# Group norm on one core: the last store of each run cut into four quarters by partitions, with waits between them, and ScalarE's loop left unaligned

## The chip, the cores and the metric

The kernel runs on one core of a Trainium2 chip. The metric is device time in microseconds (us) of one execution, lower is better. The kernel before takes 633.49 us (median of three runs, 633.39 to 634.88).

## The reference

Group norm over x of shape (128, 1024, 32, 16) in bf16, with 32 groups of 32 channels. Each of the 128 x 32 groups has 32 x 512 = 16384 values. Cut to what matters:

```python
xr  = x.reshape(B, 32, C // 32, H, W)
mu  = xr.mean(axis=(2, 3, 4), keepdims=True)
var = ((xr - mu) ** 2).mean(axis=(2, 3, 4), keepdims=True)
xn  = ((xr - mu) / jnp.sqrt(var + 1e-5)).reshape(B, C, H, W)
return xn * g[None, :, None, None] + b[None, :, None, None]
```

x is 134.2 MB and is read once; the output has the same size and is written once.

## The kernel before, in words

**Tiles.** A tile holds four samples: 4 x 32 groups lie on the 128 partitions, and each partition has the 16384 bf16 values (32 KB) of one group. A tile is 4 MB, and there are 32 of them (NT = 32). They go through six buffers in SBUF, xt0 to xt5 (NBUF = 6); tile i is in buffer i % 6. The result is written over the input in the same buffer and stored from there.

**Engines.** For each tile TensorE (L142) sums the 32 slices of 512 columns into one PSUM tile by 32 matmuls with the identity matrix. VectorE reduces that to the negative mean (L161). ScalarE makes two passes of Square with accumulation over halves of the tile (L255), then two small activations that give the standard deviation (L269, L276). VectorE takes the reciprocal (L174), forms a scale and a bias for each of the 32 channels of a group (L177, L184) and applies them by 32 instructions in place (L194). Its last instruction adds one to the semaphore s_dve.

**Loops.** TensorE, VectorE and ScalarE each run two tiles unrolled, and then a hardware loop of five trips with six tiles in its body. This is the helper `loop` (L90 to L106). It hands the loop `head_slot={engine.engine: 0}`: the loop's first instruction is loaded at slot 0 of an instruction fetch block, and a branch leads over the padding.

**SyncE and the DMA order.** All large transfers are issued by SyncE, in `sync_program` (L108 to L123), which is fully unrolled. A transfer is one tile of 128 partitions. SyncE works through its list in order, so a wait in it holds back all that stands behind it. Six loads go first. Then for each tile i SyncE waits until VectorE is done with it (s_dve, L119) and issues its store (L120), which adds 16 to the buffer's semaphore st on landing. After every third store (RUN = 3; i = 1, 4, 7, ... 25) it issues the loads of the next run, and ahead of each it waits for the landing of the store that last used the buffer (L112, L113):

```python
def load(i):
    j = i % NBUF
    if i >= NBUF:
        sync.wait_ge(st[j], 16 * (i // NBUF))
    sync.dma_start(out=xt[j][:], in_=x_v[i]).then_inc(ld[j], 16)
```

So the order is: six loads, two stores, two loads, and then three stores and three loads in turn; after the load of tile 31 come the last six stores. There are nine places at which a run of stores is followed by loads. ScalarE issues two small loads of g and b at the start.

Of the kernel before, what the change touches and what calls it, by code (L numbers as in the profile page):

```python
# [17 lines left out]
NBUF = 6  # L18
RUN = 3
# [5 lines left out]
def kernel(  # L25
# [8 lines left out]
    P = nc.NUM_PARTITIONS  # L34
# [6 lines left out]
    NT = B0 // NS  # L41
# [8 lines left out]
    o_v = out.rearrange("(t n) (g k) h w -> t (n g) (k h w)", n=NS, g=G)  # L50
# [6 lines left out]
    xt = [sb.tile([P, F], BF16, name=f"xt{j}") for j in range(NBUF)]  # L57
# [19 lines left out]
    def sem(name):  # L77
        return tc.alloc_semaphore(name)

    ld = [sem(f"ld{j}") for j in range(NBUF)]  # L80
    st = [sem(f"st{j}") for j in range(NBUF)]
    s_gb, s_set, s_eye, s_rep = sem("s_gb"), sem("s_set"), sem("s_eye"), sem("s_rep")
    s_pe, s_mean, s_sq, s_std = sem("s_pe"), sem("s_mean"), sem("s_sq"), sem("s_std")
    s_dd, s_dve = sem("s_dd"), sem("s_dve")

    def col(t, i):
        j = i % NBUF
        return t[:, j : j + 1]

    def loop(engine, step, settle, counts):  # L90


        for i in range(HEAD):
            step(i)
        with nc.Fori(
            0,
            TRIPS,
            1,
            engines=bass.OrderedEngineSet([engine.engine]),
            head_slot={engine.engine: 0},  # L100
        ):
            for i in range(HEAD, HEAD + NBUF):
                step(i)
            settle()
            for s, n in counts:
                engine.sem_inc(s, -n)  # L106

    def sync_program(sync):  # L108
# [3 lines that stand above are left out]
                sync.wait_ge(st[j], 16 * (i // NBUF))  # L112
            sync.dma_start(out=xt[j][:], in_=x_v[i]).then_inc(ld[j], 16)  # L113

        for i in range(min(NBUF, NT)):
            load(i)
        for i in range(NT):
            j = i % NBUF
            sync.wait_ge(s_dve, i + 1)  # L119
            sync.dma_start(out=o_v[i], in_=xt[j][:]).then_inc(st[j], 16)  # L120
            if (NT - NBUF - 1 - i) % RUN == 0:
                for n in range(max(NBUF, i + 1 + NBUF - RUN), min(i + 1 + NBUF, NT)):
                    load(n)  # L123

    def tensor_program(pe):
        pe.wait_ge(s_gb, 32)
        pe.wait_ge(s_rep, 1)
        pe.matmul(  # L128
            out=gb_p[:].rearrange("p a k -> p (a k)"),
            lhsT=rep[:],  # L130
            rhs=gb_b[:].rearrange("q a k -> q (a k)"),
            start=True,
            stop=True,
        ).then_inc(s_pe, 1)
        pe.wait_ge(s_eye, 1)

        def step(i):
            j = i % NBUF
            pe.wait_ge(ld[j], 16)
            pe.sem_inc(ld[j], -16)  # L140
            for k in range(NMM):
                m = pe.matmul(  # L142
                    out=pa[j][:],
                    lhsT=eye[:],
                    rhs=xt[j][:, k * MM_FREE : (k + 1) * MM_FREE],
                    start=(k == 0),
                    stop=(k == NMM - 1),
                )
            m.then_inc(s_pe, 1)

        loop(pe, step, lambda: None, [])
        pe.drain()
        pe.sem_inc(s_pe, 1)

    def vector_program(dve):
# [52 lines left out]
        def settle():  # L208
            dve.wait_ge(s_dd, 3 * (HEAD + NBUF) + 2)

        mean(0)
        loop(
            dve,
            step,
# [31 lines left out]
    def scalar_program(act):  # L246
        act.dma_start(out=gb_b[:, 0, :], in_=g_v).then_inc(s_gb, 16)
        act.dma_start(out=gb_b[:, 1, :], in_=b_v).then_inc(s_gb, 16)
        act.wait_ge(s_set, 2)
        act.activation(out=warm[:], in_=eps_t[:], func=ACT.Sqrt)  # L250

        def step(i):
            j = i % NBUF
            for h in range(2):
                m = act.activation(  # L255
                    out=ja[:],
                    in_=xt[j][:, h * F // 2 : (h + 1) * F // 2],
                    func=ACT.Square,
                    bias=col(negmean, i),
                    scale=1.0,  # L260
                    accum_out=sq[:, 2 * j + h : 2 * j + h + 1],
                    saturate=False,
                )
                if h == 0:
                    m._wait_ge(s_mean, i + 1)
                else:
                    m._wait_ge(s_sq, 3 * i + 1)
                m.then_inc(s_sq, 1)
            act.activation(  # L269
                out=col(half, i),  # L270
                in_=sq[:, 2 * j : 2 * j + 1],
                func=ACT.Identity,
                bias=eps_t[:],
                scale=inv_n,
            )._wait_ge(s_sq, 3 * i + 1).then_inc(s_sq, 1)
            act.activation(  # L276
                out=col(std, i),
                in_=sq[:, 2 * j + 1 : 2 * j + 2],
                func=ACT.Sqrt,
                bias=col(half, i),  # L280
                scale=inv_n,
            )._wait_ge(s_sq, 3 * i + 3).then_inc(s_std, 1)

        loop(act, step, lambda: act.drain(), [(s_mean, NBUF), (s_sq, 3 * NBUF)])

    with tc.tile_critical():  # L286
        with nc.Block() as block:
            block.sync(sync_program)
            block.tensor(tensor_program)
            block.vector(vector_program)  # L290
            block.gpsimd(pool_program)
            block.scalar(scalar_program)

        for j in range(NBUF):
            nc.sync.wait_ge(st[j], 16 * len(range(j, NT, NBUF)))
# [30 lines left out]
```

## Time and profile before

| | |
|---|---|
| median of three runs | 633.49 us |
| time of the profiled execution | 632.89 us |
| its span, first to last instruction | 631.1 us |
| moved to and from HBM | 134.22 MB read, 134.22 MB written, 425 GB/s over the span |
| busy: TensorE | 260.1 us, 41% |
| busy: VectorE | 375.6 us, 60% |
| busy: ScalarE | 476.2 us, 75% |
| load, issue to landing (median) | 29.1 us |
| store, issue to landing (median) | 33.3 us |

The profile is that of one execution. Its page gives busy times, the span in 40 equal slices (each digit is a busy share in tenths), the DMA queues, the chain of work that ended last, and groups of instructions by source line with the mean duration of one in nanoseconds. The trace behind it answers who waited for whom, prints instructions in order of time, and records every DMA packet with its start, duration and size, and the landing of every transfer. Times in the trace count from the span's start. SyncE has no busy time: all that it does is wait and issue.

### The profile page before, as it was taken

The numbers are of one execution on the slowest core, as the hardware profiler recorded it, in microseconds if no ns is written. First come the engines' busy times: TensorE is split into PE (matmuls) and PEld (weight loads), VectorE is DVE, ScalarE is ACT, GpSimd is POOL, SyncE is SP. The second block draws the span as 40 slices with busy tenths as digits, with TensorE's granted clock in tenths as the row PEclk, the third lists the DMA queues.
The fourth block names the chain that finished last, engine by engine and source line by source line (L and its number), as shares of the span: only waits on it lengthen the run. The fifth ranks groups of instructions, "written<-read, shape, count | busy, mean of one in ns | idle before, by whom it ended". The sixth has DMA issues, their size and how long they took to land. (4 is left out here: it accounts for less than half of the span.)

```text
span 631.1 us, 3670 instructions
## 1 busy us (share of the span) xinstructions
PE 260.1 (41%) x1025; PEld 106.2 (17%) x1025; DVE 375.6 (60%) x1188; ACT 476.2 (75%) x194; POOL 0.9 (0%) x7
## 2 busy tenths in 40 slices
PE   1877409008602750572087018604720670095000
PEld 0333103003201310230032003201310230032000
DVE  0067477774772777077627745770777177447771
ACT  0596999996994699199819965993899199749940
POOL 0000000000000000000000000000000000000000
PEclk9988858658855975687578659755975796588555
DMA  8999999999999999999999999999999999999996
GB/s 366 431 432 402 434 434 432 435 432 432 430 432 434 434 432 434 432 432 434 432 432 430 432 434 430 432 434 432 426 436 434 434 428 434 432 436 432 432 397 287
DMA packets 9320, 268.53 MB, mean 425 GB/s; under 512 B 1120, under 2 KB 1120, under 8 KB 1120
## 3 DMA queue, kind: packets, MB, share of 16 engines
q1 hardware_dynamic: 9216, 268.44, 99.0%
q14 instruction: 6, 0.05, 0.0%
q8 instruction: 2, 0.03, 0.0%
q10 hardware_dynamic: 96, 0.00, 0.0%
HBM read 134.22 MB, written 134.22 MB: 425 GB/s over the span
## 5 line engine op out<-in xcount | busy, mean ns | idle before, releaser
L255 ACT ACTIVATE ja<-xt,negmean 128x8192 fp8e5<-128x8192 bf16 x64 | 455.5, 7117 | 127.1 <-DVE jd L161 120.6
L142 PE MATMUL pa<-xt,eye 128*128 128x512 bf16 x1024 | 259.9, 419 | 309.1 <-PEq L140 306.9
L194 DVE TENSOR_SCALAR xt<-xt,scl,bia 128x512 bf16<-128x512 bf16 x1024 | 333.6, 405 | 1.2
L142 PEld LDWEIGHTS pa<-xt,eye 128*128 128x128 bf16 x1024 | 106.1, 106 | 462.5 <-issue 368.8
L161 DVE TENSOR_SCALAR_CACHE_REDUCE jd<-pa 128x512 bf16<-128x512 f32 x33 | 22.6, 685 | 144.6 <-PE pa L142 142.8
L174 DVE RECIPROCAL rstd<-std 128x1 f32<-128x1 f32 x32 | 5.2, 162 | 82.9 <-ACT std L276 82.9
L255 ACT ACTIVATION_READ_ACCUMULATOR ja<-xt,negmean 128x1 f32 x64 | 11.9, 186 | 0.0
L276 ACT ACTIVATE std<-sq,half 128x1 f32<-128x1 f32 x32 | 9.4, 294 | 1.0
L269 ACT ACTIVATE half<-sq,eps_t 128x1 f32<-128x1 f32 x32 | 8.9, 278 | 0.0
L184 DVE SCALAR_TENSOR_TENSOR bia<-scl,negmean,gb 128x32 f32<-128x32 f32 x32 | 8.0, 251 | 1.1
L177 DVE TENSOR_SCALAR scl<-gb,rstd 128x32 f32<-128x32 f32 x32 | 7.7, 242 | 1.1
L157 DVE COPY gb<-gb_p 128x64 f32<-128x64 f32 x1 | 0.2, 225 | 9.8 <-PE gb_p L128 9.8
L128 PE MATMUL gb_p<-gb_b,rep 32*128 32x64 bf16 x1 | 0.2, 231 | 10.8 <-DMA gb_b<-in_b_dram 10.8
L250 ACT ACT_TABLE_LOAD x1 | 1.3, 1283 | 1.9 <-issue 1.9
L161 DVE DVE_READ_ACCUMULATOR jd<-pa 128x1 f32 x33 | 2.7, 81 | 0.0
L128 PEld LDWEIGHTS gb_p<-gb_b,rep 32*128 32x128 bf16 x1 | 0.1, 100 | 10.8 <-DMA gb_b<-in_b_dram 10.8
L156 DVE MEMSET ones_b<- 128x128 bf16 x1 | 0.2, 165 | 1.1 <-SPq L286 1.1
L229 POOL TENSOR_SCALAR_AFFINE_SELECT rep<-ones_b 32x128 bf16<-32x128 bf16 x1 | 0.3, 305 | 0.0
L220 POOL TENSOR_SCALAR_AFFINE_SELECT eye<-ones_b 128x128 bf16<-128x128 bf16 x1 | 0.3, 294 | 0.8 <-DVE ones_b L156 0.8
L250 ACT ACTIVATE warm<-eps_t 128x1 f32<-128x1 f32 x1 | 0.2, 203 | 0.0
L238 POOL TENSOR_SCALAR eps_t<-ones_b 128x1 f32<-128x1 bf16 x1 | 0.2, 204 | 0.0
L310 POOL MEMSET const-bfloat16-1.0<- 128x1 bf16 x1 | 0.1, 102 | 0.0
(3 smaller groups left out, 0.3 us busy)
## 6 DMA issues: line engine op xcount, KB each, us to landing
xt<-in_x_dram SPq DMA_DIRECT2D x32, 4096.0 KB, 29.1
out_dram<-xt SPq DMA_DIRECT2D x32, 4096.0 KB, 33.3
gb_b<-in_g_dram ACTq DMA_DIRECT2D x1, 2.0 KB, 6.1
gb_b<-in_b_dram ACTq DMA_DIRECT2D x1, 2.0 KB, 9.3
```

Source lines behind the costliest of these rows:

```text
L128: pe.matmul(out=gb_p[:].rearrange("p a k -> p (a k)"), lhsT=rep[:], rhs=gb_b[:].rearrange("q a k -> q (a k)"), start=True, stop=True,).the ...
L142: m = pe.matmul(out=pa[j][:], lhsT=eye[:], rhs=xt[j][:, k * MM_FREE : (k + 1) * MM_FREE], start=(k == 0), stop=(k == NMM - 1),)
L161: dve.tensor_scalar(out=jd[i % 2][:], in0=pa[i % NBUF][:], scalar1=-inv_n, scalar2=None, op0=ALU.mult, op1=ALU.add, accum_out=col(negmean, i),
L174: dve.reciprocal(out=col(rstd, i), in_=col(std, i))._wait_ge(s_std, i + 1).then_inc(s_dd, 1)
L177: dve.tensor_scalar(out=scl[j][:], in0=gam, scalar1=col(rstd, i), scalar2=None, op0=ALU.mult,)._wait_ge(s_dd, 3 * i + 2).then_inc(s_dd, 1)
L184: dve.scalar_tensor_tensor(out=bia[j][:], in0=scl[j][:], scalar=col(negmean, i), in1=bet, op0=ALU.mult, op1=ALU.add,)._wait_ge(s_dd, 3 * i ...
L194: m = dve.tensor_scalar(out=span, in0=span, scalar1=scl[j][:, k : k + 1], scalar2=bia[j][:, k : k + 1], op0=ALU.mult, op1=ALU.add,)
L220: pool.affine_select(out=eye[:], in_=ones_b[:], pattern=[[-1, P]], compare_op=ALU.is_equal, fill=0.0, base=0, channel_multiplier=1,)._wait ...
L250: act.activation(out=warm[:], in_=eps_t[:], func=ACT.Sqrt)
L255: m = act.activation(out=ja[:], in_=xt[j][:, h * F // 2 : (h + 1) * F // 2], func=ACT.Square, bias=col(negmean, i), scale=1.0, accum_out=s ...
L269: act.activation(out=col(half, i), in_=sq[:, 2 * j : 2 * j + 1], func=ACT.Identity, bias=eps_t[:], scale=inv_n,)._wait_ge(s_sq, 3 * i + 1) ...
L276: act.activation(out=col(std, i), in_=sq[:, 2 * j + 1 : 2 * j + 2], func=ACT.Sqrt, bias=col(half, i), scale=inv_n,)._wait_ge(s_sq, 3 * i + ...
```

## The change

Two edits.

In `sync_program`, the store at each of the nine places where loads follow (i = 1, 4, ... 25) is replaced by four stores of 32 partitions each, 1 MB, with three new semaphores qt0 to qt2. The first two quarters are issued together; the third is issued when the first has landed, and the fourth when the second has landed. The fourth adds to st as the whole store did. Then SyncE waits for the landing of the third, and goes on to the loads, whose own waits are as before. The other 23 stores stay whole.

In `loop`, ScalarE's loop is built without `head_slot`: its body is loaded right behind the unrolled part, wherever in a block that is. The instructions of the body are the same, and those of the other engines are all as before.

```diff
+    qt = [sem(f"qt{c}") for c in range(3)]
...
-    def loop(engine, step, settle, counts):
+    def loop(engine, step, settle, counts, aligned=True):
...
-            head_slot={engine.engine: 0},
+            **({"head_slot": {engine.engine: 0}} if aligned else {}),
...
+        def gated(i):
+            return i < NT - NBUF and (NT - NBUF - 1 - i) % RUN == 0
+
+        def store_in_quarters(i):
+            j = i % NBUF
+            q = P // 4
+            n = 16 * (gates[0] + 1)
+            gates[0] += 1
+            for c in range(4):
+                if c >= 2:
+                    sync.wait_ge(qt[c - 2], n)
+                rows = slice(c * q, (c + 1) * q)
+                sync.dma_start(out=o_v[i][rows], in_=xt[j][rows]).then_inc(
+                    qt[c] if c < 3 else st[j], 16
+                )
+            sync.wait_ge(qt[2], n)
+
+        gates = [0]
...
-            sync.dma_start(out=o_v[i], in_=xt[j][:]).then_inc(st[j], 16)
+            if gated(i):
+                store_in_quarters(i)
+            else:
+                sync.dma_start(out=o_v[i], in_=xt[j][:]).then_inc(st[j], 16)
...
-        loop(act, step, lambda: act.drain(), [(s_mean, NBUF), (s_sq, 3 * NBUF)])
+        loop(act, step, lambda: act.drain(), [(s_mean, NBUF), (s_sq, 3 * NBUF)], aligned=False)
```

## The prediction

> **What bounds the kernel now.** I read the page's DMA part first, then the windows by stage, then SyncE's waits and its timeline, and the chain last. On the page the DMA row, the rate row and the queue row:
>
> ```profile
> DMA  8999999999999999999999999999999999999996
> GB/s 366 431 432 402 434 434 432 435 432 432 430 432 434 434 432 434 432 432 434 432 432 430 432 434 430 432 434 432 426 436 434 434 428 434 432 436 432 432 397 287
> q1 hardware_dynamic: 9216, 268.44, 99.0%
> ```
>
> The reader is to see nines from the second slice to the last but one, and 426 to 436 from the fifth slice to the third from the end: SyncE's queue keeps the 16 DMA engines busy for 99% of the span. 9216 packets are 144 a transfer: 128 rows of 32 KB and 16 short ones that report completion. In the trace's packet records 95 of 100 rows take 1213 to 1219 ns, load or store alike, so one engine moves 27.0 GB/s, and a transfer (8 rows an engine) takes 8 x 1.213 = 9.70 us. Landings do follow each other by 9.69 us. Two windows, one steady cycle of three loads and three stores and the stretch before the first store (columns: length, busy time of each engine, clock, DMA share, GB/s):
>
> ```profile
> 53.20:64.40 11.20, 8.75 (x32) 3.50 (x32) 10.98 (x34) 6.59 (x1) 0.00 (x0) 0.85 1.00 383
> 249.10:307.90 58.80, 24.34 (x96) 9.99 (x96) 35.90 (x114) 45.24 (x19) 0.00 (x0) 0.73 1.00 431
> ```
>
> In the cycle DMA is full (1.00), while ScalarE, the busiest engine, has 45.2 of 58.8 us. So whatever lengthens the DMA work of a cycle lengthens the kernel by as much, and compute has 13 us a cycle to spare. What keeps DMA full is depth in the queue, seen in SyncE's timeline of a cycle (start, length from first issue to last, line):
>
> ```profile
> 221.26 0.33 SPq L120 DMA_DIRECT2D out_dram<-xt  x1
> 229.80 19.65 SPq L113 DMA_DIRECT2D xt<-in_x_dram  x3
> 249.50 30.17 SPq L120 DMA_DIRECT2D out_dram<-xt  x3
> ```
>
> and in its waits (who <- for what: us in total, times, longest):
>
> ```profile
> SPq L120 <- DVE xt L194: 368.3, 23, 44.6
> SPq L113 <- DMA out_dram<-xt: 223.3, 25, 10.1
> ```
>
> The run's last store is issued at 221.26 with two stores ahead of it and lands at 249.11. The next loads are issued at 229.80, 239.50 and 249.12, on the landings of the three stores, so the first load stands 19 us in the queue before its data can flow. At the end, the chain:
>
> ```profile
> 607.00 10.42 DVE xt L194 x32
> ```
>
> VectorE ends at 617.42, the last store is issued at 617.44, and the store ahead of it lands at 619.51: compute and DMA reach the end within about a microsecond of each other (15 DMA engines write their last row until 628.0, one until 628.86). Both chains start at the landings of the last three loads, so a delay ahead of those goes to the end in full.
>
> **The change part by part.** All sums are against the profiled execution, 632.89 us, which lies 0.6 us under the median of 633.49.
>
> *Bytes and packets.* Nothing is removed: a quarter is 32 rows. The two small loads of g and b, also 32 rows, show how such a transfer is spread: 64 data packets and 32 completion packets for the two, so 32 and 16 each, two rows on every one of 16 engines. The nine places have 27 more issues and 27 x 16 completion packets of 9 ns, three to an engine and place: under 0.3 us in all, and the issues (0.33 us) lie beside data. Nothing.
>
> *The waits.* SyncE now waits for a first quarter, a second and a third; behind it stand the remaining quarters, the loads, and the next run's stores. The next stores are not late: before, SyncE came to them at the landing of the whole store (249.50) as well, and three loads (29 us) then cover them. The loads lose their 19 us of cover and keep one quarter. The price of a hand-over, from the end of one quarter's data to the first packet of the next, in the rows: completion packet to landing 0.34 to 0.46 us, landing to SyncE's issue 0.01 (store landed 249.11, load issued 249.12), issue to first packet 1.02 (first load, 1.00 to 2.02): 1.4 us. The worst row is the g load, issue 0.96 to first packet 3.93, behind other data: 2.97, in all 3.4. The cover is the quarter that is still in flight, at least 2 x 1.213 = 2.43 us. So at 1.4 us nothing shows; at 3.4 us it costs 3 hand-overs x 1.0 us x 9 = 27 us.
>
> *The length of a quarter.* This decides. Lower end: each engine keeps its 1213 ns a row, a quarter takes 2.43 us, four take 9.70, as the whole store did: zero. But a whole store has the 16 engines reading 16 sets of eight rows, and a quarter has them all reading within 32 partitions. No transfer of size in the trace does that. Loads write SBUF and read HBM, stores do the reverse, and both run at 1213 ns: the limit is not HBM's reading or writing but the engine's own, or that of its way into SBUF. If it is the way, two engines that meet on one share it: 2 x 1.213 = 2.43 us a row, 4.85 a quarter, 19.41 for four against 9.69, 9.72 more at each of nine places: **+87.5 us**. Upper end: the slowest row in the records, 2.508 us (at 58.8, in the 383 GB/s window above, where many engines slow down at once): 5.02 a quarter, 20.06 for four, +10.4 x 9 = +93 us. I take 4.85, the doubled row; its row of 2.43 us is nearest to the slow rows that the trace does have, 2.1 to 2.5 us. In it the hand-overs are covered by 4.85 us.
>
> [...]
>
> *ScalarE's loop.* At the loop's entry ScalarE stands idle, with nothing that released it:
>
> ```profile
> 52.06 0.29 ACT L276 ACTIVATE std<-sq,half 128x1 f32<-128x1 f32 x1
> 57.81 7.12 ACT L255 ACTIVATE ja<-xt,negmean 128x8192 fp8e5<-128x8192 bf16 x1 [5.45 <-issue]
> ```
>
> Two 8 KB instruction packets run at 56.1. Without the jump up to 5.45 us go from ScalarE's path; tile 2's store is next held by SyncE, which issues it at 84.12, right behind a load at 83.74, and DMA is full throughout: zero. On the other side, a body that straddles two blocks could stall as long at each of four back edges. ScalarE waits there 5.0 us (146.8) and 13.4 to 13.6 (from 254.6 on) for VectorE anyway, which covers it but for 0.45 us that DMA does not see. Were that cover gone, in the last cycle, it would be 5.45 us. Value: zero.
>
> **Sum**: 632.89 + 87.5 = **720.4 us**.
>
> **Rivals.**
>
> *No change.* The rows keep 1213 ns, because the limit is the engine's own. Then 9.70 against 9.69 at each place, hand-overs of 1.4 us under 2.43: 633 us. For it: 27.0 GB/s in all rows of both directions. Against: it asks that 32 partitions feed 16 engines as 128 do.
>
> *Faster* (the other side). The engines drift apart: the completion packets of the store that landed at 249.11 are spread over 3.05 us, of that at 542.07 over 5.46. The third load of a run lands late, by 0.69, 0.77, 0.40 and 0.40 us (278.88, 395.9, 454.46, 513.03), when the leading engines are already at stores; one landing at 123.27 is 0.77 late. A gate stops the leaders until the last engine has landed a quarter, and closes the spread at each of nine places, while the last engine always has a quarter in hand. If the late landings come from the spread, 3.0 us go: 629.9 us. It decides only where a quarter lasts under 2.43 + 3.0 / 36 = 2.51 us. Against: the late loads come only at some of the places, while the spread is there at all.
>
> *Hand-overs uncovered.* Rows at full rate, but a hand-over near 3.4 us: 633 + 27 = 660 us. Against: the 3.4 is behind another queue's rows.
>
> **How the numbers follow.** The doubled row 0.58 (by itself 705 to 732: down to 0.83 x 87.5 = 73 us more, if drift keeps two engines of a way apart for a sixth of the rows, and up to 726 plus one ScalarE stall of 5.45), hand-overs or a row in between 0.08, no change 0.16, faster 0.18. About 0.3% (1.9 us) is what a measurement of this kernel can tell from no change. Faster 0.18, same 0.16, slower 0.66. The likeliest alone holds too little, so the range reaches over the cases between and no change to the edge of the faster one, 630, and up to 732.
>
> **What would show it.** In the profile after: DMA share stays near 1.00 while the rate falls to about half in a stretch of some 19 us at each place, and SyncE's wait between the second and third quarter is near 4.85 us. A flat 430 with waits of 2.43 us would be no change; then the spread and the third loads' landings tell of the faster rival. A DMA share under 0.9 ahead of the loads would be uncovered hand-overs. The prediction is wrong if a row of a quarter stays at 1213 ns.

## The result, and the profile after

The kernel after takes 722.12 us (median of six runs, 719.67 to 726.4) against 633.92 us before (six runs): a ratio of 1.1397, 95% interval 1.1355 to 1.1439. The forecast was 720.4 us. The profiled execution after has 724.91 us and a span of 723.2 us, 92.1 us more than the span before; all that follows is told against these two spans.

The DMA row, the rate row and the queue row of the page after:

```profile
DMA  9999999999999999999999999999999999899997
GB/s 377 434 433 404 241 411 425 270 341 419 435 219 379 406 430 228 417 426 370 259 431 430 317 314 428 410 299 338 428 431 241 391 433 393 219 428 406 435 433 323
q1 hardware_dynamic: 9648, 268.44, 98.0%
```

The DMA row is still nines but for one 8 and the last slice, and the rate row is no longer flat: it dips at nine places, to between 219 and 314, one for each cut store. The DMA engines are nearly as busy as before and move about half as much there. A busy share alone would not have shown this; share and rate have to be read together. The 432 added packets (9648 against 9216) are the completions.

One place by windows, after (columns: length, busy time of each engine, clock, DMA share, GB/s): the four quarters, from the landing of the store ahead of them to their own last landing; within that, the last quarter; then the first load behind them.

```profile
270.80:287.80 17.00, 0.00 (x0) 0.00 (x0) 11.09 (x35) 15.12 (x8) 0.00 (x0) 0.50 0.94 220
283.80:287.90 4.10, 0.00 (x0) 0.00 (x0) 0.00 (x0) 2.18 (x4) 0.00 (x0) 0.50 0.76 216
287.80:299.60 11.80, 0.00 (x0) 0.00 (x0) 0.00 (x0) 0.00 (x0) 0.00 (x0) 0.50 0.99 394
```

A whole last store, and the first load behind it, in the kernel before:

```profile
239.50:249.10 9.60, 0.00 (x0) 0.00 (x0) 8.95 (x29) 9.54 (x5) 0.00 (x0) 0.50 1.01 437
249.10:258.80 9.70, 0.00 (x0) 0.00 (x0) 2.13 (x7) 5.74 (x4) 0.00 (x0) 0.50 1.00 432
```

The same 4 MB take 17.0 us at 220 GB/s where they took 9.6 at 437. The load behind them takes 11.8 instead of 9.7. A window counts each packet whole at its start, so share and rate of a short one are rough, and shares over 1 occur. The 0.76 of the last quarter leaves out rows that began before it. With every row counted by the part of it that lies inside, the engines are 0.91 busy there and idle for 0.4 us; in the whole 17.0 us they are idle for 0.5.

SyncE's timeline at this place, and its waits for landings in the whole span (us in total, times, longest):

```profile
252.41 26.66 SPq L130 DMA_DIRECT2D out_dram<-xt  x4
283.78 4.40 SPq L114 DMA_DIRECT2D xt<-in_x_dram  x3
```

```profile
SPq L130 <- DMA out_dram<-xt: 220.2, 18, 25.7
SPq L114 <- DMA out_dram<-xt: 59.4, 18, 4.8
```

The first load is now issued at 283.78, when the third quarter has landed, 4.1 us before the last one lands; before, it was issued 19 us ahead.

ScalarE at its loop's entry, after:

```profile
52.99 0.29 ACT L300 ACTIVATE std<-sq,half 128x1 f32<-128x1 f32 x1
53.20 7.11 ACT L279 ACTIVATE ja<-xt,negmean 128x8192 fp8e5<-128x8192 bf16 x1
```

The 5.45 us stall is gone.

**Where the 92 us are.** The landing records give a sum. Over the nine places the quarters take 67.8 us more than whole stores at 9.69 us would (17.2 us a place); the first loads behind them land 18.7 us late in all (2.1 each); all other landings together are 5.5 us later than before; the first load lands 0.3 us later. That is 92.3, the difference of the spans to 0.2 us. The packet records give a second sum, per DMA engine: 512 rows at 1.213 us are 621.1 us; rows that took longer added 3.0 us before and 86.7 after; time with no row in work was 2.8 us before and 11.5 after. Before, nearly all of that lies at the end, where engines that are ahead wait for the last store, issued at 617.44; after, 8.8 us of it lie at the nine places. So about nine tenths are slow rows, and one tenth is idle time. 580 rows took 2.50 to 2.60 us (the quarters have 1152); before, one did.

### The profile page after: what moved, and what is told of

Read it like the earlier page. It is cut to its first block, busy times and chain, and to the rows that moved or that the text cites. A ratio compares the mean times of both kernels' runs of the same rounds, so it can differ in the third digit from the quotient of the medians.

```text
span 723.2 us, 3705 instructions
## 1 busy us (share of the span) xinstructions
PE 259.1 (36%) x1025; PEld 105.8 (15%) x1025; DVE 375.8 (52%) x1188; ACT 476.1 (66%) x194; POOL 0.9 (0%) x7
## 3 DMA queue, kind: packets, MB, share of 16 engines
q1 hardware_dynamic: 9648, 268.44, 98.0%
## 5 line engine op out<-in xcount | busy, mean ns | idle before, releaser
L279 ACT ACTIVATE ja<-xt,negmean 128x8192 fp8e5<-128x8192 bf16 x64 | 455.5, 7116 | 217.9 <-DVE jd L185 216.9
L152 PE MATMUL gb_p<-gb_b,rep 32*128 32x64 bf16 x1 | 0.2, 230 | 11.1 <-DMA gb_b<-in_b_dram 11.1
L152 PEld LDWEIGHTS gb_p<-gb_b,rep 32*128 32x128 bf16 x1 | 0.1, 99 | 11.1 <-DMA gb_b<-in_b_dram 11.1
## 6 DMA issues: line engine op xcount, KB each, us to landing
out_dram<-xt SPq DMA_DIRECT2D x36, 1024.0 KB, 11.2
```

Source lines behind the costliest of these rows:

```text
L152: pe.matmul(out=gb_p[:].rearrange("p a k -> p (a k)"), lhsT=rep[:], rhs=gb_b[:].rearrange("q a k -> q (a k)"), start=True, stop=True,).the ...
L279: m = act.activation(out=ja[:], in_=xt[j][:, h * F // 2 : (h + 1) * F // 2], func=ACT.Square, bias=col(negmean, i), scale=1.0, accum_out=s ...
```

## The experiments

The theory on record: two DMA engines that read within the same group of partitions share one way into SBUF, so that a row takes twice its time. Its rivals: the waits empty the queue; the cutting itself costs; ScalarE's loop has a part in it; closing the spread between the engines helps. Times are medians; ratios are against the kernel before, run beside it on the same chip. This table has the sums of the two records in the profiled execution, for all kernels but e4 (mean over the nine places; slow rows and idle time per engine over the span):

| kernel | us | ratio, 95% interval | last store of a run, us | load behind it, us | slow rows, us | idle, us |
|---|---|---|---|---|---|---|
| before | 633.9 | | 9.7 | 9.7 | 3.0 | 2.8 |
| e1 loop only | 633.7 | 0.9994 (0.9985 to 1.0003) | 9.7 | 9.7 | 2.6 | 3.3 |
| after | 722.1 | 1.1397 (1.1355 to 1.1439) | 17.2 | 11.8 | 86.7 | 11.5 |
| e2 quarters only | 721.1 | 1.1358 (1.1328 to 1.1388) | 16.7 | 11.8 | 85.7 | 8.4 |
| e3 by columns | 645.7 | 1.0177 (1.0163 to 1.0191) | 9.8 | 10.3 | 18.0 | 3.0 |
| e7 every fourth partition | 648.8 | 1.0240 (1.0226 to 1.0255) | 9.7 | 10.5 | 16.3 | 5.7 |
| e6 halves | 705.6 | 1.1145 (1.1124 to 1.1165) | 15.5 | 10.9 | 70.5 | 8.4 |
| e5 middle 64 and two 32 | 676.6 | 1.0673 (1.0658 to 1.0689) | 12.0 | 11.2 | 43.7 | 6.7 |
| e11 eighths of 16 | 807.7 | 1.2724 (1.2699 to 1.2750) | 25.9 | 12.6 | 151.2 | 29.8 |
| e9 order changed | 698.7 | 1.1037 (1.0995 to 1.1078) | 14.2 | 12.0 | 59.4 | 10.4 |
| e10 columns, no waits | 636.6 | 1.0055 (1.0041 to 1.0068) | 9.8 | 9.7 | 6.1 | 3.6 |
| e8 eighths by columns | 660.0 | 1.0408 (1.0389 to 1.0428) | 10.6 | 11.1 | 22.3 | 9.4 |
| e12 one gate | 635.2 | 1.0017 (1.0008 to 1.0027) | 9.8 (one place) | 10.3 | 4.8 | 2.4 |

### Each edit alone: e1 and e2

e1 is the kernel before with only the `head_slot` of ScalarE's loop taken away; e2 is the kernel after with it put back:

```diff
-        loop(act, step, lambda: act.drain(), [(s_mean, NBUF), (s_sq, 3 * NBUF)], aligned=False)
+        loop(act, step, lambda: act.drain(), [(s_mean, NBUF), (s_sq, 3 * NBUF)])
```

> ScalarE's loop without alignment, all stores whole. If the time comes from the quarters alone: the 5.45 us stall at ScalarE's loop entry is gone and DMA does not notice, 633 to 634 us, ratio 1.000 within 0.003. If the unaligned loop has a share in it: above 636 us, with stalls of ScalarE at the loop's back edges.

> The quarters with all waits, ScalarE's loop aligned as before. Quarters alone: 720 to 724 us as with both edits, and the 5.45 us stall at ScalarE's loop entry is back without effect. If the loop has a share: clearly off 722.

e1 took 633.68 us, e2 721.11. In e2 the stall is back:

```profile
52.45 0.29 ACT L300 ACTIVATE std<-sq,half 128x1 f32<-128x1 f32 x1
57.87 7.12 ACT L279 ACTIVATE ja<-xt,negmean 128x8192 fp8e5<-128x8192 bf16 x1 [5.12 <-issue]
```

and the time is that of the change. So the loop is worth nothing that can be told from noise, alone or beside the quarters, and the quarters are the whole of it.

### Rows or columns: e3

The quarters keep their bytes, number and waits, and have 128 partitions:

```diff
-            q = P // 4
+            q = F // 4
...
-                rows = slice(c * q, (c + 1) * q)
-                sync.dma_start(out=o_v[i][rows], in_=xt[j][rows]).then_inc(
+                cols = slice(c * q, (c + 1) * q)
+                sync.dma_start(out=o_v[i][:, cols], in_=xt[j][:, cols]).then_inc(
```

> Both edits, but a quarter is 128 partitions by 4096 columns instead of 32 partitions by 16384: the same bytes, number of transfers, waits and cover. Theory of shared ways (engines that read the same group of partitions share one way): each engine has its own group again, a quarter takes 2.4 us, hand-overs of 1.4 us are covered, 632 to 636 us; if closing the spread between engines helps, 630. Theory of waits (the hand-overs empty the queue): still 700 to 722 us.

645.68 us: 76 of the 88 us are gone with every wait in place, and the idle time is back at 3.0 us (2.7 of it at the places, 2.4 at two of the nine). The four quarters of one place, in a window from landing to landing:

```profile
295.10:304.90 9.80, 0.18 (x1) 0.00 (x0) 7.24 (x23) 9.77 (x5) 0.00 (x0) 0.63 0.96 411
```

9.8 us for 4 MB, and the records give 2.41 to 2.48 us between the quarters' landings. The theory of waits falls. The expected 632 to 636 was missed by 10 us, though, and the 630 of the spread theory by more: e10 and e12 go after that.

### The quarters without their waits: e4

All four are issued one behind the other and add to the buffer's own semaphore, and the loads wait for its total.

```diff
+            gated = i < NT - NBUF and (NT - NBUF - 1 - i) % RUN == 0
+            for rows in PIECES if gated else [slice(0, P)]:
+                sync.dma_start(out=o_v[i][rows], in_=xt[j][rows]).then_inc(st[j], 16)
+                due[j] += 16
```

> ScalarE's loop unaligned, the same four quarters by partitions, issued one behind the other with no wait between them and none ahead of the loads but for their own on the landing of the whole tile's store (all four quarters add to its semaphore). Theory of shared ways: a quarter still takes 4 to 5 us, and only what the waits add goes (about 2 us at each of nine places), 700 to 718 us. Theory of waits: 634 us.

720.45 us, in four executions that lie between 707 and 757 us, so no ratio is given. The theory of waits falls here as well. The expected gain of some microseconds at each place did not come either. The profiled execution has fewer slow rows than the change (72.3 us against 86.7) and more idle time (18.8 against 11.5): the digits of its DMA row, 9 before, end in 8, 6 and 5. Leading engines run ahead unchecked there: the 16 landings of the last load of a run lie 7.2 us apart at the first place and 17.0 at the last, and 13.6 us of the idle time lie in the last six stores. Why the executions differ so much was not settled.

### Which partitions: e6, e5, e7, e11

The same chain of waits (each piece behind the landing of the last but one, the loads behind the last but one), with other pieces:

```diff
+PIECES = [slice(0, 64), slice(64, 128)]                           # e6
+PIECES = [slice(32, 96), slice(0, 32), slice(96, 128)]            # e5
+PIECES = [slice(c, 128, 4) for c in range(4)]                     # e7
+PIECES = [slice(16 * c, 16 * c + 16) for c in range(8)]           # e11
...
-            for c in range(4):
+            for c, rows in enumerate(PIECES):
...
```

> Two pieces of 64 partitions, 0 to 63 and 64 to 127, instead of four of 32; both issued at once, the loads gated on the landing of the first. Base: quarters by columns with all waits took 646 us, by 32 partitions 722. Theory A (what counts is the number of partitions, and 64 are enough): 640 to 650 us. Theory B (64 neighbouring partitions give half the rate as 32 do): 705 to 725 us. [...]

> Three pieces: partitions 32 to 95, then 0 to 31, then 96 to 127, with the same rule of waits (each piece behind the landing of the last but one, loads behind the landing of the second). Theory A (64 partitions are enough, whichever): half the excess over 646, about 684 us. Theory B1 (any 64 partitions give half the rate): 705 to 725 us. Theory B2 (it depends on which 64): about 684 us with halves at 720. [...]

> Four quarters of 32 partitions as in the change, with the same waits, but quarter c takes every fourth partition, c, c + 4, ... 124, so that each quarter is spread over all 128. Theory 'reach' (only the set of partitions that the transfer touches counts): 640 to 650 us. Theory 'meeting' (what counts is which partitions are read at the same moment; with two neighbouring rows an engine, engines 0 and 4 read partitions 0 and 32 and so on in step, and meet if those share a way): 700 to 725 us.

> Eight pieces of 16 neighbouring partitions, chained as the quarters are (each behind the landing of the last but one, loads behind the seventh). Theory of shared ways: 16 neighbours reach four ways, so four engines share one, a row takes up to 4 x 1.213 = 4.85 us and eight pieces up to 38.8 us; with the overlap seen in the quarters (68 us of a possible 87 showed) 840 to 910 us. Rival: neighbouring rows cost a fixed factor of two, or the wait does: 720 to 740 us.

The stored tile of one place, in windows of e6, of e5 (first piece, then the other two), of e7 and of e11, in this order:

```profile
398.90:414.30 15.40, 0.00 (x0) 0.00 (x0) 11.08 (x35) 15.30 (x10) 0.00 (x0) 0.50 0.95 260
```

```profile
508.30:513.10 4.80, 0.00 (x0) 0.00 (x0) 4.76 (x15) 4.80 (x1) 0.00 (x0) 0.50 0.98 403
513.10:519.60 6.50, 0.00 (x0) 0.00 (x0) 5.91 (x19) 6.47 (x3) 0.00 (x0) 0.50 0.99 242
```

```profile
364.70:374.40 9.70, 0.00 (x0) 0.00 (x0) 9.35 (x30) 9.67 (x4) 0.00 (x0) 0.50 1.03 419
```

```profile
376.00:401.50 25.50, 0.00 (x0) 0.00 (x0) 11.08 (x35) 15.81 (x10) 0.00 (x0) 0.50 0.88 153
```

Halves of 64 neighbours are slow too: 260 GB/s, and the rows over 2.24 us (a line drawn here, well over the 1.213 of most rows) have a median of 2.55. So it is not the number of partitions. Partitions 32 to 95, also 64 neighbours, land 2 MB in 4.8 us (4.84 to 4.88 at seven of the nine places), which is the full rate, and the two 32s behind them fall to 242 GB/s. So it depends on which 64. The 676.6 us lie 7 under the 684 on record. Quarters that take every fourth partition, 32 rows of 32 KB as in the change, run at the full rate: 9.70 us for four, rows at 1.213 us. That is the forecast of "reach", and "meeting" falls in the form it was put on record in, with two neighbouring rows an engine. How the rows are dealt out to the engines was not seen, so a meeting under another deal is not excluded. Eighths of 16 neighbours are slower than quarters: 153 GB/s, and the rows over 2.24 us have a median of 3.41 and a maximum of 5.05 us. The direction is the theory's, the size is less than the 840 to 910 us on record. Why it is less was not tested; here too two pieces are in flight, and e9 below shows that what is beside a piece changes its rate (14.2 us a place against 17.2).

Taken together: pieces within partitions 0 to 63, or within 64 to 127, ran at 260 GB/s and less (halves 260, quarters 220 in the change and 242 in e5, eighths 153), where a whole tile runs at 437, and pieces with a part in both ran at the full rate. Partitions 32 to 95 landed 2 MB in 4.8 us, half the time of a whole tile; the strided quarters of e7, which reach from one end of the 128 to the other, took 2.43 us each. So all 128 partitions were not needed for it. Rows of 2.55 us, where those of a whole tile take 1.213, fit two engines on one way; no record shows a way, so the sharing remains the theory's explanation.

One rival was not varied by itself: in every cut the places in HBM that are written move along with the partitions. The size of the piece there is not it, since e6 and e5 both write 2 MB in one stretch, at 260 GB/s and at the full rate. A limit in HBM that goes by address, as the rate here goes by partition, stays possible; these runs cannot tell the two apart.

### The order of the quarters: e9

```diff
+PIECES = [slice(0, 32), slice(64, 96), slice(32, 64), slice(96, 128)]
```

> The change's quarters and waits, but in the order 0-31, 64-95, 32-63, 96-127, so that the two in flight use different ways whenever engines are out of step. Theory of shared ways: leading engines start the second piece while the others read the first, at more than half rate, so the four take less than the 17.1 us mean of the change: 690 to 715 us. If a quarter's rate is its own whatever is beside it: 720 to 724 us.

698.7 us, 14.2 us a place instead of 17.2. One place by window:

```profile
393.20:406.90 13.70, 0.00 (x0) 0.00 (x0) 11.04 (x35) 13.67 (x3) 0.00 (x0) 0.50 0.92 251
```

With the same pieces and waits, only the neighbour in the queue has changed, so the rate of a quarter does depend on what is beside it: slow rows cost 59.4 us here and 86.7 in the change. In the change too the second and third quarter, 32 to 63 and 64 to 95, may overlap where engines are out of step; e5 landed these two at the full rate (2 MB in 4.8 us). That its quarters took 17.2 us and not 19.4 has a second reason, though: when the store ahead lands, the leading engines have already done 23 of the quarters' 128 rows, and when the last quarter lands, only 11 of the load's (means of the nine places). So part of the quarters' time falls ahead of the window, and the load behind starts with less done and lands late.

### What the waits cost by themselves: e10, e8, e12

e10 (shown against the kernel before) has the quarters by columns with no waits between, and the loads only behind their own; e8 (against e3) has eighths by columns with all waits; e12 (against e3) has quarters by columns at tile 13 alone:

```diff
+            q = F // 4 if gated else F                                        # e10
+            for c in range(F // q):
+                cols = slice(c * q, (c + 1) * q)
+                sync.dma_start(out=o_v[i][:, cols], in_=xt[j][:, cols]).then_inc(st[j], 16)
+                due[j] += 16
...
-            q = F // 4                                                        # e8
+            q = F // 8
...
-            return i < NT - NBUF and (NT - NBUF - 1 - i) % RUN == 0           # e12
+            return i == 13
```

> ScalarE's loop unaligned, the gated stores as four quarters by columns issued one behind the other, no waits between and none ahead of the loads but their own. With all waits this took 646 us, 11.5 more than before, most of it in late landings at the first load behind the stores and at the third load. If the waits cost it, by bringing the engines back into step at each gate: 633 to 635 us. If the cutting itself costs it (8 KB rows, 27 more transfers): 643 to 647 us.

> Eight pieces by columns (128 partitions by 2048), chained, so that only 1.2 us of data cover a hand-over. Hand-overs of 1.4 us: uncovered by some 0.2 us or more at seven places of each of nine gates, the DMA engines show idle time ahead of pieces, 655 to 675 us. If the 12 us that quarters by columns cost were uncovered hand-overs already, twice as many of them with half the cover: above 690 us. If a hand-over costs nothing here: 644 to 648 us.

> Quarters by columns with all waits at one place only, the store of tile 13; the other eight are whole as before. Theory of step (engines brought into step make each change of direction dearer, about 1 us a change, and drift makes it cheap again): the spread of the engines falls to about 1 us at that place, the next third load lands about 1 us late, then less; 634 to 636 us. If the spread has nothing to do with it: nothing late behind the place beyond what the kernel before shows.

Against the kernel before, e3 is 11.5 us slower and e10 2.9 (by the medians; 0.55% by the ratio). e10's 636.6 us lies between its two expectations. So the waits cost close to 9 us and the cutting about 3, although the waits add hardly any idle time: e3 has 3.0 us of it and 18.0 of slow rows, e10 3.6 and 6.1. With half the cover, e8, the idle time does appear: 9.4 us, and the landings of its pieces alternate between about 1.25 and 1.4 us, where an eighth of 9.70 is 1.21. The hand-over therefore lies between the two covers, above 1.2 and below 2.4 us, as the 1.4 us of the prediction has it.

The slow rows of e3 lie where the direction of the traffic changes: the first load behind the quarters lands 0.65 us late on average, and the last load of the run, with stores behind it, 0.67 to 1.47 us late at every place; before, five of those nine loads land on time. The spread of their 16 completion packets is 0.65 to 2.2 us in e3 and 2.3 to 5.5 before. e12 shows both in one execution. Its second and third load behind the gate, and the same third load in the kernel before:

```profile
318.00:327.80 9.80, 9.26 (x32) 3.56 (x32) 0.30 (x1) 0.00 (x0) 0.00 (x0) 0.76 1.01 435
327.80:338.50 10.70, 7.07 (x32) 3.06 (x32) 10.59 (x35) 10.24 (x3) 0.00 (x0) 1.00 1.02 398
```

```profile
327.30:337.00 9.70, 7.24 (x34) 3.06 (x32) 9.27 (x30) 8.61 (x3) 0.00 (x0) 1.00 1.01 432
```

The load before the change of direction runs at 435, the one at it at 398, at a full DMA share. The spread there is 1.15 us (3.5 us at the place before), and that load is 1.00 us late; at the four places behind it the spread grows to 1.5, 2.0, 2.2 and 2.6 us and the loads are 0.3 to 0.4 late. The theory of step forecast this, but the spread alone does not set the lateness. At the first place behind the gate of e12 the load ahead has a spread of 1.15 us, and the last load is 0.3 late; in e3 the last loads behind a spread of 1.1 to 1.3 us are 1.3 to 1.5 late, and those behind a smaller spread, 0.5 to 1.0 us, 0.7 to 1.2. e10 has spreads of 3.0 to 6.9 us and a last load that is 1.0 late. So the gates make the loads behind them late (e3 against e10, and e12 at its one gate); why they do, and what slows the rows at the change, was not measured.

## Why the prediction was right, point by point

**What bounds the kernel.** Right: DMA was full in the kernel before (its queue busy for 99.0% of the span), so time added there came out in full, 92 us in the span.

**Bytes and packets at nothing.** Nearly: cutting by columns costs 2.9 us (e10). For whole rows of 32 KB the cutting alone was not tried.

**The waits at nothing.** Right in the mechanism: a hand-over of 1.4 us is covered by 2.43 (e3), and is not by 1.2 (e8). Two things were not in the sum. The first is idle time, 8.8 us at the nine places: 4.7 in the first two quarters, 0.6 in the third and 3.5 in the last. A quarter has landed only when its slowest engine is done, and until then just one more is in the queue, so engines that come in far ahead run dry. Where the 16 landings of the store ahead lie 5.4 us apart, the first two quarters lose 2.1 us; at two places with 4.4 us they lose 1.0; at the other six, with 2.3 to 3.6 us, 0.2 at most. The second is that the waits make the loads behind them late; e3 against e10 prices that at close to 9 us, and the cause stays open.

**The length of a quarter at 4.85 us.** The step that decided, and it held: rows of 2.55 us, just over the 2.43 taken. Of the cause named, e3, e6, e5 and e7 show that the rate goes by the partitions that a piece takes (short of the place in HBM, which moved along); that two engines share a way into SBUF was not shown. By landings a place costs 7.5 us, not 9.72, and the first load behind it 2.1, which I had at nothing: 9.6 together. The split between the two depends on how far the leading engines are ahead (see e9), so the packet records are the better sum. Had all 1152 rows taken 2.55 us, they would have added 96.3 us an engine, 8.8 more than the 87.5. Slow rows added 83.7, at least 12.6 less than that, which goes with an overlap of the second and third quarter (e9); the range allowed for such an overlap, the sum did not. Idle time added 8.7. So the 87.5 came out as 92.4 because the row that was taken too short and the idle time left out outweigh the overlap by little. 720.4 is therefore closer to 722 than its terms deserve, and that part is luck.

**ScalarE's loop at nothing.** Right: 0.9994 (0.9985 to 1.0003), with the stall gone. A stall at the back edges, for which the range had 5.45 us, was not shown: in the kernel after, all idle time of ScalarE but the 1.9 us at its start is put down to VectorE (216.9 us in nine waits).

**Rivals.** *No change* fell by the rows of 2.55 us. *Hand-overs uncovered* fell by e3's idle time. *Faster* had its first half right where rows run at full rate, since in e3 the gates do close the spread, and its second half wrong: with the spread closed, the last loads of the runs land later, by 9.7 us in all against 2.3 before.

**What would show it.** The rate fell to half over 17.0 us, with the share at 0.94. The sign for SyncE was put wrongly: it issues the third quarter 12 us (at the first place) to 27 us behind the second, because whole stores, up to two, still stand ahead of the quarters in the queue. It is the landings of the second and third quarter that lie 5.0 us apart (mean of nine).

## What to carry to other kernels

Here a DMA that was cut kept its rate where its pieces stayed spread over the partitions (64 in the middle, 32 to 95, were spread enough: 2 MB in 4.8 us): the same quarters cost 14% as blocks of 32 neighbours and about 2% as columns or as every fourth partition, waits included. Read DMA share and rate side by side; here a nearly full share at half the rate (0.94 and 220 GB/s) was rows of 2.55 us instead of 1.213 and not a queue that ran dry. And read idle time in a short stretch from the packets' own starts and ends. A wait on a landing can add hardly any idle time and still cost (close to 9 us in e3, for a reason left open); here the version without any gate remained the fastest, and no kernel tried beat it clear of its interval.

## What the runs showed of the hardware that was not expected

Strided quarters (every fourth partition) reach the full rate, 1.213 us a row, so for that rate the partitions of a transfer did not have to be neighbours here, or all 128. Drift between the DMA engines is little loss in the kernel before: with engines spread by 2.3 to 5.5 us the last load of a run lands 0 to 0.8 us late; gates that bring them to within 2.2 us (e3) go with 0.7 to 1.5 us. Drift costs where a gate meets it: in the change, engines that come to the quarters 4.4 to 5.4 us apart are idle there for 1 to 2 us on average. And cutting by partitions with nothing to pace it (e4) left the time itself uncertain, 707 to 757 us in four executions, where every paced kernel stayed within 1%.
